# Attention backward on one core: dq columns as a stream of four a head, and dV three heads ahead of dK

## The chip, the cores and the metric

The kernel runs on one core of a Trainium2 chip. Its time is in microseconds of the device, the median of several executions. Besides it there is one profiled execution, from which all views of the trace come; its span is counted from the first to the last instruction. The engines are named as the profile names them: PE (TensorE, with PEld for its weight loads), DVE (VectorE), ACT (ScalarE), POOL (GpSimd) and SP (SyncE, which here only issues DMAs).

## The reference

One decode step of a transformer block is computed forward and then backward. The forward part, cut to what matters:

```python
# x [4,1,512], k_cache and v_cache [4,32,4096,128], all bf16
q = (layernorm(x) @ wq) per head                  # 4 x 32 heads of 128
p = softmax(q . k_cache * 128**-0.5)              # over 4096 keys
o = p . v_cache
h = x + o @ wo
out = h + (silu(hn @ w1) * (hn @ w3)) @ w2        # hn = layernorm(h)
```

The outputs are `out` and the gradients of x, k_cache, v_cache, wq, wo, w1, w3 and w2 for a given `grad_out`. For one head, with dO the gradient of its output o:

- dV = p (x) dO, an outer product of 4096 x 128 (1 MB in bf16)
- dS = p * (dO . V - c) * scale, with c = dO . o
- dK = dS (x) q, again 4096 x 128
- dq = scale * (M^T dO - c * kP), where M is the sum over keys of p * v k^T and kP the sum of p * k, both made in the forward part; dq then gives the gradients of wq and x.

## The kernel before

There are 128 heads (4 batches by 32), numbered s = 0 to 127. The keys and values of a head are 1 MB each. The front (lines 604 to 676) reads all K and V once and computes, a pair of heads at a time, scores, softmax (P_all), the matrix M of each head (128 x 129 in fp32) and kP. A middle stretch (lines 678 to 924) does the output projection, the second layernorm, the feed-forward part and its backward, down to dO of the first 32 heads (page 0), and makes dV of heads 0 and 1. The back (from line 927) reads all V a second time and writes dK and dV of all heads, and does all the rest beside that.

**Slots.** SBUF holds 23 slots of 1 MB (`Slot`, line 108), handed out from a queue of free ones. In the back, M occupies eight (16 heads each), the pages of wo up to four, one holds replicated rows, seven circulate among the second loads of V (`vring`, NV2 = 7, lines 789 to 798), and the others take dV and dK on their way out (`gv`, `gk`): such a slot is given back at once, and its next user waits for the DMA.

**The head pass.** `front(s)` (line 1161) turns the V of head s round: 32 transposes on PE in four batches, each evicted by ACT into the same slot (`V_T`, lines 757 to 765), then eight matmuls dO . V (line 1177), whose stationary operand `zd` POOL prepares two heads before (line 1142). After every fourth head the sums are evicted, transposed once more (lines 1152 and 1159), and `group_dS` (line 1185) makes dS of four heads on DVE.

**Outer products.** `grad_V(s)` (line 777) and `grad_K(s)` (line 1197) are one DVE instruction each (line 770), followed by a DMA of 1 MB on SP's queue (lines 781 and 1201). dV needs only P (pairs of P made by POOL, line 1147, three buffers) and the dO row of the head, replicated over the partitions; dK needs dS and the replicated q row. `replicate` (line 1121) makes such rows for four heads: four matmuls on PE into one PSUM buffer, one eviction on ACT.

**Order.** The program's order is written out by hand (lines 1233 to 1265), and each engine, SP's DMA queue among them, takes its own instructions in that order. Before the main loop, heads 0 to 4 pass `front`, and `more_V` (line 1212) makes dV of heads 2 to 8 between them. In the main loop over s, at each s: SP loads a further head of V into the slot that the last head pass set free; `front(s + 5)`; dV up to head s + 8 (`lead_V`, line 1224: the distance shrinks to 3 between heads 56 and 76); dK of head s; after every fourth head dS of the next four; one or more steps of work beside it.

**Work beside it.** It is written as generators and advanced by `step`. The generator "o" (line 1105, heads 2 to 20) transposes the remaining pages of wo and makes dO of heads 32 to 127, a page of 32 heads in six steps; its last step on a page has POOL put dO into `dOT_f` as fp32 (line 750). The generator "s" (`side_work`, line 951) begins at head 21 with three steps a head until head 35, then two. Its first 43 steps make dq: one fp32 matmul of 128 x 128 by one column for each head, three heads a step, so nine a head; every 16 heads one slot of M is given back, and after 64 and 96 heads a load of a quarter of wq is issued on SP's queue. What follows in "s" (dx, gradients of the weights, the output itself) takes about 150 steps.

Of the kernel before, what the change touches and what calls it, by code (L numbers as in the profile page):

```python
# [9 lines left out]
FP32 = mybir.dt.float32  # L10
# [14 lines left out]
def kernel(  # L25
# [22 lines left out]
    nc = tc.nc  # L48
    P = nc.NUM_PARTITIONS
# [5 lines left out]
    Dh = A_k_cache.shape[3]  # L55
    F = B_w1.shape[1]
    NH = B * H
    HD = H * Dh
    assert NH == P and Dh == P and H == 32 and Sk == 32 * P
    assert D == 4 * P and F % P == 0  # L60
    DC = D // P
# [5 lines left out]
    MC = 16  # L67
# [3 lines left out]
    x2 = A_x.rearrange("b s d -> (b s) d")  # L71
# [12 lines left out]
    def bh_of(s):  # L84
        return s % B, s // B

    def rows_of(ap):
        return ap.rearrange("(p j) d -> p j d", p=P)
# [74 lines left out]
    ident_b = const.tile([P, P], BF16, name="ident_b")  # L163
# [14 lines left out]
    def ones_window(col):  # L178
# [11 lines left out]
                          in_=rowg[:, None, :, None].to_broadcast([P, 4, 8, 4]))  # L190
# [70 lines left out]
    with ExitStack() as c0:  # L261
# [11 lines left out]
        for h in range(H):  # L273
            for cc in range(DC):
                nc.tensor.matmul(qT_ps[:, h, :], lhsT=wq_s[cc].b(HD)[:, h * Dh:(h + 1) * Dh], rhs=xhatT[:, cc, :],
                                 start=(cc == 0), stop=(cc == DC - 1))
# [4 lines left out]
        for r in range(2):  # L281
            for t_ in range(2):
                for q in range(4):
                    nc.tensor.matmul(qr_ps[32 * q:32 * (q + 1), 2 * r + t_, :], lhsT=ident_b[:, 64 * r + t_:64 * (r + 1):2],
                                     rhs=qT_bf[:], start=True, stop=True, tile_position=(0, 32 * q))
# [3 lines left out]
    Ms = []  # L289

    def M_of(s):
        return Ms[s // MC].f(MC * (Dh + 1)).rearrange("p (n c) -> p n c", c=Dh + 1)[:, s % MC, :]
# [305 lines left out]
    units = {"d": d_hh_units()}  # L598

    def step(k, n=1):  # L600
        for _ in range(n):
            next(units[k], None)
# [113 lines left out]
    dOT_f = pers2.tile([P, NH], FP32, name="dOT_f")  # L716
    dOrows_bf = pers2.tile([NH, Dh], BF16, name="dOrows_bf")
# [4 lines left out]
    qrows_bf = pers2.tile([NH, Dh], BF16, name="qrows_bf")  # L722
# [29 lines left out]
    REP = B  # L752
    reps = {}
# [13 lines left out]
    P2s, first_gv = {}, []  # L767
# [9 lines left out]
    def grad_V(s):  # L777
        b, h = bh_of(s)
        gv = Slot("gv")
        outer(gv.heads(), P2s.pop(s), reps["rdo", s // REP][:, s % REP, :])  # L780
        nc.sync.dma_start(out=rows_of(out_3[b, h]), in_=gv.heads())
        if s > 1:
            gv.give()
        else:
            first_gv.append(gv)
# [14 lines left out]
    with ExitStack() as cm:  # L800
# [33 lines left out]
        for wi, wt in enumerate((w1, w3)):  # L834
            for fc in range(FC):
                for cc in range(DC):
                    nc.tensor.matmul(gu_ps[:, wi, fc, :], lhsT=w13_view(wt, cc)[:, fc * P:(fc + 1) * P], rhs=hhatT[:, cc, :],
                                     start=(cc == 0), stop=(cc == DC - 1))
# [25 lines left out]
        for jj in range(DC):  # L864
            i_mm = 0
            for (lt, wt) in ((d_gateT_bf, w1), (d_upT_bf, w3)):
                for fc in range(FC):
                    nc.tensor.matmul(dn_ps[:, jj, :], lhsT=w13_view(wt, jj)[:, fc * P:(fc + 1) * P], rhs=lt[:, fc, :],
                                     start=(i_mm == 0), stop=(i_mm == 2 * FC - 1))
                    i_mm += 1  # L870
        for sl in w1 + w3:
            sl.give()
        rs = Slot("reps")
        rep_bufs = {nm_: [rs.b()[:, (2 * k + i) * 512:(2 * k + i + 1) * 512].rearrange("p (i d) -> p i d", i=REP) for i in range(2)]
                    for k, nm_ in enumerate(("rq", "rdo"))}
# [4 lines left out]
        ps = psA.tile([P, REP, Dh], FP32, tag="rT", name="repq_ps")  # L880
# [4 lines left out]
        for s in range(3):  # L885
# [8 lines left out]
                         start=True, stop=True)  # L894
# [14 lines left out]
        for b0, b1 in ((0, 1), (1, B)):  # L909
            ps = psA.tile([P, B, Dh], FP32, tag="rT", name="rep_ps")  # L910
            for b in range(b0, b1):
                for jj in range(DC):
                    nc.tensor.matmul(ps[:, b, :], lhsT=dhT[:, jj, b:b + 1].to_broadcast([P, P]), rhs=wo_page(0)[:, 0, jj, :],
                                     start=(jj == 0), stop=(jj == DC - 1))
# [12 lines left out]
    with ExitStack() as c2:  # L927
        psT = c2.enter_context(tc.tile_pool(name="psT2", bufs=2, space=bass.MemoryType.PSUM))
        psD = c2.enter_context(tc.tile_pool(name="psD", bufs=1, space=bass.MemoryType.PSUM))
        psrep = c2.enter_context(tc.tile_pool(name="psrep", bufs=1, space=bass.MemoryType.PSUM))  # L930
        psg = c2.enter_context(tc.tile_pool(name="psg", bufs=2, space=bass.MemoryType.PSUM))
        psx = c2.enter_context(tc.tile_pool(name="psx", bufs=1, space=bass.MemoryType.PSUM))
# [15 lines left out]
            gu.append((dst, ps, n))  # L948


        def side_work():
            pt = psg.tile([P, Dh], BF16, tag="gps", name="pt_O")
            nc.tensor.transpose(pt[:], OT_bf[:], ident_b[:])
            nc.scalar.copy(out=O_sb[:], in_=pt[:])
            dq_ps = psx.tile([P, 512], FP32, tag="x2", name="dq_ps")
            wq2s = deque()

            def load_wq2(cc):
                if cc < DC:
                    wq2s.append(Slot("wq2"))  # L960
                    nc.sync.dma_start(out=wq2s[-1].b(HD), in_=A_wq[cc * P:(cc + 1) * P, :])

            for s in range(NH):
                nc.tensor.matmul(dq_ps[:, s:s + 1], lhsT=M_of(s)[:, 0:Dh], rhs=dOT_f[:, s:s + 1], start=True, stop=True)
                if s % MC == MC - 1:
                    Ms[s // MC].give()
                    if s // MC in (3, 5):
                        load_wq2(s // MC // 2 - 1)
                if s % 3 == 2:
                    yield  # L970
            yield
            t = rs.f(2080)[:, 1536:1536 + NH]
            nc.vector.tensor_tensor(out=t, in0=c_rep[:], in1=kPT[:], op=ALU.mult)
# [13 lines left out]
            for cc in range(DC):  # L987
                wq2 = wq2s.popleft()
# [8 lines left out]
                for h in range(H):  # L997
                    nc.tensor.matmul(dx_ps[0:B, cc * P:(cc + 1) * P], lhsT=dqT_bf[:, h * B:(h + 1) * B], rhs=wv[:, h, :],
                                     start=(h == 0), stop=(h == H - 1))
# [62 lines left out]
            for i in range(2):  # L1062
                st = Slot("gw2")
                hw = hh_rows[:, i * 7 * P:(i + 1) * 7 * P].rearrange("b (p k) -> b k p", k=7)
                for k in range(7):
# [4 lines left out]
                                  in_=st.b(7 * D).rearrange("p (c j) -> p c j", c=7))  # L1070
# [4 lines left out]
            for (rows, out_ap) in ((dg_rows, out_6), (du_rows, out_7)):  # L1075
                for i in range(2):
                    st = Slot("gw13")
                    nw = hhat_bf[0:B, i * 2 * P:(i + 1) * 2 * P].rearrange("b (p k) -> b k p", k=2)
                    for k in range(2):
                        for (f0_, w_) in f_chunks:  # L1080
# [5 lines left out]
                                      in_=st.b(2 * F).rearrange("p (c f) -> p c f", c=2))  # L1086
                    st.give()
            r1.give()
            for h0 in range(0, H, 8):
                st = Slot("gwo")  # L1090
                ow = oflat.b(HD)[0:B, h0 * P:(h0 + 8) * P].rearrange("b (p k) -> b k p", k=8)
                for k in range(8):
# [4 lines left out]
                                  in_=st.b(8 * D).rearrange("p (k j) -> p k j", k=8))  # L1097
# [20 lines left out]
            nc.scalar.copy(out=dh, in_=dr_ps[:])  # L1118

        units["o"] = rest_of_dO()  # L1120
        def replicate(nm_, i0):
            if i0 >= NH or (nm_, i0 // REP) in reps:
                return
            K_ = 8 * B if i0 < 8 * B else P
            rows = dOrows_bf if nm_ == "rdo" else qrows_bf
            ps = psrep.tile([P, REP, Dh], FP32, tag="rep", name="rep_ps")
            for i in range(REP):
                nc.tensor.matmul(ps[:, i, :], lhsT=ident_b[0:K_, i0 + i:i0 + i + 1].to_broadcast([K_, P]), rhs=rows[0:K_, :],
                                 start=True, stop=True)
            rt = rep_bufs[nm_][i0 // REP % 2]  # L1130
            nc.scalar.copy(out=rt, in_=ps[:])
            reps[nm_, i0 // REP] = rt

        rows = {}
        dS2s = {}
# [8 lines left out]
        def P_pairs(s):  # L1144
            if s < NH and s not in P2s:
                P2s[s] = bw3.tile([P, SJ, 2], BF16, tag="P2", name="P2")
                nc.gpsimd.tensor_copy(out=P2s[s][:], in_=P_all[:, s, :, None].to_broadcast([P, SJ, 2]))  # L1147
# [13 lines left out]
        def front(s):  # L1161
            hl = s % B
            if s not in VTs:
                for g in range(SJ // GW):
                    V_T(s, psT, range(g, g + 1))
                    if hl == 0 and g == 0:
                        rows_out()
                    if hl == 0 and g == 2:
                        rows_T()
            VT = VTs[s].heads()  # L1170
            if hl == 0:
                rows["acc"] = psD.tile([P, 512], FP32, tag="dP", name="dP_ps")
            dO_window(s + 2)
            for u in range(2):
                for c in range(4):
                    j0 = 8 * c + 4 * u
                    nc.tensor.matmul(rows["acc"][32 * c:32 * (c + 1), :], lhsT=zq_window(zd[hl], 2 * hl + u),  # L1177
                                     rhs=VT[:, j0:j0 + 4, :], start=(hl == 0 and u == 0),
                                     stop=(hl == B - 1 and u == 1), tile_position=(0, 32 * c))
            if hl == B - 1:  # L1180
                rows["ps"] = rows.pop("acc")
            sl = VTs.pop(s)
            (vring if len(V2s) + len(VTs) + len(vring) < NV2 else free).append(sl.i)
# [22 lines left out]
                load_V2(nc.sync)  # L1206


        O0, S0, L = 2, 21, 5
        gvd = {"n": 2}  # L1210

        def more_V(upto):
            while gvd["n"] < min(NH, upto):
                s = gvd["n"]
                P_pairs(s)
                replicate("rdo", s - s % REP)
                grad_V(s)
                P_pairs(s + 1)
                P_pairs(s + 2)
                gvd["n"] += 1  # L1220
                if s % REP == 2:
                    replicate("rdo", s + 2)

        def lead_V(s):
            return 8 - min(5, max(0, s - 56) // 4)


        def load_ahead(s):
            prefetch()
            if s < NH and s not in V2s and s not in VTs:  # L1230
                load_V2(nc.sync)

        for s in range(2):
            dO_window(s)
        for s in range(3, 6):
            P_pairs(s)
        for s in range(L):
            load_ahead(s)
            front(s)
            if s == 0:  # L1240
                for gv in first_gv:
                    gv.give()
            more_V((4, 6, 7, 8, 9)[s])
            if s == 0:
                replicate("rdo", REP)
        group_dS(0)
        for s in range(NH):
            load_ahead(s + L)
            if s % REP == 2:
                replicate("rq", s + 2)  # L1250
            if s + L < NH:
                front(s + L)
            elif s + L == NH:
                rows_out()
                rows_T()
            if s > 0:
                more_V(s + 1 + lead_V(s))
            grad_K(s)
            if s % B == B - 1 and s + 1 < NH:
                group_dS((s + 1) // B)  # L1260
            if s >= S0:
                step("s", 3 if s < S0 + 15 else 2)
            elif s >= O0:
                step("o")
        step("s", 400)


# [28 lines left out]
```

## Time and profile before

| | |
|---|---|
| median of 3 runs | 1703.83 us (1702.63 to 1705.36) |
| profiled execution | 1702.63 us |
| its span | 1700.7 us |
| PE busy | 1258.0 us (74%) |
| DVE busy | 1236.7 us (73%) |
| ACT busy | 967.2 us (57%) |
| POOL busy | 397.8 us (23%) |
| moved by DMA | 707.50 MB, mean 416 GB/s |
| HBM read, written | 422.59 MB, 282.34 MB |
| second V load, dV, dK | 128 DMAs of 1 MB each |

The page cuts the span into 40 slices of 42.5 us and gives for each the busy tenths of the engines, of the 16 DMA engines and the GB/s moved. The front fills slices 0 to 15, the back begins in slice 16 near 703 us, and its main loop near 726 us. Views by window give, for a stretch, the time in it, the busy time of PE, PEld, DVE, ACT and POOL with the number of instructions, then the granted clock of PE, the DMA share and GB/s. Views in order of time give start, duration, engine, line, operation and count of merged instructions, and in brackets the idle time before and what ended it. For an instruction of SP, the duration is that of the issue, not of the transfer; the landing of each transfer is told by its semaphore.

### The profile page before, as it was taken

How to read it: one execution, taken by the hardware profiler on the slowest of the kernel's cores; microseconds unless marked ns; L12 is line 12 of the kernel's file. 1: busy time of each engine (PE TensorE's matmuls, PEld its weight loads, DVE VectorE, ACT ScalarE, POOL GpSimd, SP SyncE). 2: the span in 40 equal slices, each digit the busy share in tenths (PEclk: the TensorE clock that was granted, in tenths of full speed). 3: DMA queues.
4: the chain of work that ended last, by engine and by line, in shares of the span. 5: the costliest groups of instructions: out<-in, count | busy, mean ns of one | idle time of the engine just before them, and what ended most of it. 6: DMA issues, size and time to landing. Idle time of an engine off the chain costs nothing. (4 is left out here: it accounts for less than half of the span.)

```text
span 1700.7 us, 38400 instructions
## 1 busy us (share of the span) xinstructions
PE 1258.0 (74%) x16180; PEld 931.3 (55%) x16180; DVE 1236.7 (73%) x1294; ACT 967.2 (57%) x1502; POOL 397.8 (23%) x678
## 2 busy tenths in 40 slices
PE   5889888888888888877689877676577666666660
PEld 4777776666666666644467655443344343443440
DVE  5989899999998997667676676675465666665672
ACT  3555444544454444687754567676577666666550
POOL 1211222222222231323122352031022233200210
PEclk9999999999999999899976789988787877777665
DMA  9999999999999999999999999999999999999996
GB/s 401 424 425 423 424 424 424 423 424 424 414 424 411 422 406 401 385 419 425 425 425 426 425 424 425 425 426 426 424 422 422 419 421 415 419 421 410 412 425 280
DMA packets 101741, 707.50 MB, mean 416 GB/s; under 512 B 11052, under 2 KB 15288, under 8 KB 17600
## 3 DMA queue, kind: packets, MB, share of 16 engines
q1 hardware_dynamic: 101152, 704.95, 99.4%
q8 instruction: 127, 2.08, 0.5%
q14 instruction: 46, 0.38, 0.1%
q0 software_dynamic: 416, 0.10, 0.0%
HBM read 422.59 MB, written 282.34 MB: 414 GB/s over the span
## 5 line engine op out<-in xcount | busy, mean ns | idle before, releaser
L765 ACT COPY V<-pt_tps 128x1024 bf16<-128x1024 bf16 x512 | 490.5, 1027 | 168.0 <-PE pt_tps L764 158.7
L764 PE MATMUL pt_tps<-ident_b,V 128*128 128x128 bf16 x4096 | 361.8, 250 | 150.1 <-ACT V L765 93.1
L764 PEld LDWEIGHTS <-V 128*128 128x128 bf16 x4096 | 308.4, 114 | 258.3 <-issue 169.7
L770 DVE TENSOR_TENSOR gv<-P,reps 128x4096 bf16<-128x4096 bf16 x125 | 286.1, 2292 | 172.1 <-DMA out_dram<-gv 132.8
L770 DVE TENSOR_TENSOR gk<-dS,reps 128x4096 bf16<-128x4096 bf16 x128 | 293.4, 2294 | 111.1 <-DMA out_dram<-gv 77.3
L421 DVE TENSOR_TENSOR PK<-Kn,PK 128x4096 bf16<-128x4096 bf16 x128 | 292.3, 2283 | 26.1 <-POOL PK L417 25.7
L436 PE MATMUL M_ps<-PK,Vn 128*128 128x130 bf16 x4096 | 285.3, 222 | 33.9 <-DMA Vn<-in_A_v_cache_dram 33.4
L436 PEld LDWEIGHTS <-Vn 128*128 128x128 bf16 x4096 | 253.1, 99 | 53.8 <-DMA Vn<-in_A_v_cache_dram 45.7
L328 DVE STREAM_TRANSPOSE KT<-Kn 128x512 f32<-128x512 f32 (+1 forms) x321 | 250.6, 797 | 0.3 <-issue 0.2
L323 ACT COPY KT<-pt_tps 128x1024 bf16<-128x1024 bf16 x128 | 129.4, 1012 | 186.2 <-PE pt_tps L322 150.5
L1177 PE MATMUL dP_ps<-V,zd 128*32 128x512 bf16 x1024 | 179.1, 432 | 68.6 <-ACT V L765 65.8
L1147 POOL COPY P<-P_all 128x64 bf16<-128x64 bf16 x125 | 92.4, 740 | 468.7 <-DVE gv L770 468.6
L1142 POOL COPY zd<-dOT_bf 128x2 bf16<-128x2 bf16 x128 | 130.5, 1021 | 156.3 <-PE dP_ps L1177 156.3
L334 POOL TENSOR_TENSOR W<-qrep,wmask 128x128 bf16<-128x128 bf16 x128 | 123.7, 966 | 82.4 <-PE S_ps L354 67.6
L417 POOL COPY PK<-P_all 128x64 bf16<-128x64 bf16 x128 | 32.5, 254 | 414.6 <-ACT P_all L411 411.6
L1177 PEld LDWEIGHTS <-zd 128*32 128x32 bf16 x1024 | 37.2, 95 | 156.3 <-issue 141.7
L411 ACT COPY P_all<-pt_P 32x64 bf16<-32x64 bf16 x256 | 51.9, 203 | 53.4 <-PE pt_P L407 51.2
L322 PE MATMUL pt_tps<-ident_b,Kn 128*128 128x128 bf16 x1024 | 80.5, 223 | 0.0
L446 PE MATMUL kP_ps<-PK,onesw 128*32 128x512 bf16 x1024 | 79.1, 386 | 0.0
L322 PEld LDWEIGHTS <-Kn 128*128 128x128 bf16 x1024 | 62.0, 100 | 25.8 <-issue 25.8
L386 ACT ACTIVATE E<-S_ps,nm 128x256 f32<-128x256 f32 x64 | 30.3, 474 | 80.1 <-DVE nm L383 80.1
L400 ACT ACTIVATE Pn<-E,rl 128x1024 bf16<-128x1024 f32 x64 | 73.7, 1152 | 3.3 <-DVE rl L397 3.2
(239 smaller groups left out, 1244.8 us busy)
## 6 DMA issues: line engine op xcount, KB each, us to landing
Kn<-in_A_k_cache_dram SPq DMA_DIRECT2D x128, 1024.0 KB, 15.3
Vn<-in_A_v_cache_dram SPq DMA_DIRECT2D x128, 1024.0 KB, 15.8
V<-in_A_v_cache_dram SPq DMA_DIRECT2D x128, 1024.0 KB, 20.0
out_dram<-gv SPq DMA_DIRECT2D x128, 1024.0 KB, 20.0
out_dram<-gk SPq DMA_DIRECT2D x128, 1024.0 KB, 20.1
wq<-in_A_wq_dram SPq DMA_DIRECT2D x8, 1024.0 KB, 15.7
out_dram<-gw SPq DMA_DIRECT2D x6, 896.0 KB, 19.9
wo<-in_A_wo_dram SPq DMA_DIRECT2D x4, 1024.0 KB, 11.4
```

The lines of the kernel that those rows point to most:

```text
L322: nc.tensor.transpose(pt[:, i, :], Kn[:, c * GW + i, :], ident_b[:])
L323: nc.scalar.copy(out=KT[:, c * GW:(c + 1) * GW, :], in_=pt[:])
L328: nc.vector.transpose(out=KT[:, c * w_:(c + n) * w_], in_=Kn[:, c * w_:(c + n) * w_])
L334: nc.gpsimd.tensor_tensor(out=W[:, hl], in0=qrep[:, :, s:s + 1].to_broadcast([P, 4, 32]), in1=wmask[:, hl, None, :].to_broadcast([P, 4, 32 ...
L421: nc.vector.tensor_tensor(out=PK[:, :, 0:Dh].rearrange("p j (r t) -> p j r t", t=2), in0=Ks[s].heads().rearrange("p j (r t) -> p j r t", t=2),
L436: nc.tensor.matmul(hold["M"][:], lhsT=Vn[:, j, :], rhs=PK[:, j, :], start=(j == 0), stop=(j == SJ - 1))
L764: nc.tensor.transpose(pt[:, i, :], v[:, g * GW + i, :], ident_b[:])
L765: nc.scalar.copy(out=v[:, g * GW:(g + 1) * GW, :], in_=pt[:])
L770: nc.vector.tensor_tensor(out=dst.rearrange("p j (r t) -> p j r t", t=2), in0=col2[:, :, None, :].to_broadcast([P, SJ, Dh // 2, 2]), in1=r ...
L1142: nc.gpsimd.tensor_copy(out=zd[s % B][:, 32:132:67], in_=dOT_bf[:, s:s + 1].to_broadcast([P, 2]))
L1147: nc.gpsimd.tensor_copy(out=P2s[s][:], in_=P_all[:, s, :, None].to_broadcast([P, SJ, 2]))
L1177: nc.tensor.matmul(rows["acc"][32 * c:32 * (c + 1), :], lhsT=zq_window(zd[hl], 2 * hl + u), rhs=VT[:, j0:j0 + 4, :], start=(hl == 0 and u ...
```

## The change

Two things are rewritten. The dq columns leave `side_work` and become a generator "q" of their own, with four heads a step and one step at each head from 2 to 33; the two first loads of wq are issued after 96 and 112 heads of it. `side_work` begins at head 35 with two steps a head. And dV is no longer made up to eight heads ahead: before the main loop dV of heads 2 and 3 is made, and in the loop dV of head s + 3 beside dK of head s. With it go `more_V` and `lead_V`; the replicated rows of dO and q for four heads are now made together, at every fourth head, and P's pairs are made once at each head, five heads ahead.

```diff
+        wq2s = deque()
+
+        def load_wq2(cc):
+            if cc < DC:
+                wq2s.append(Slot("wq2"))
+                nc.sync.dma_start(out=wq2s[-1].b(HD), in_=A_wq[cc * P:(cc + 1) * P, :])
+
+        dq_ps = psx.tile([P, 512], FP32, tag="x2", name="dq_ps")
+
+        def dq_work():
+            for s in range(NH):
+                nc.tensor.matmul(dq_ps[:, s:s + 1], lhsT=M_of(s)[:, 0:Dh], rhs=dOT_f[:, s:s + 1], start=True, stop=True)
+                if s % MC == MC - 1:
+                    Ms[s // MC].give()
+                    if s // MC in (5, 6):
+                        load_wq2(s // MC - 5)
+                if s % 4 == 3:
+                    yield
+
+        units["q"] = dq_work()
+
         def side_work():
...
-            for s in range(NH):
-                nc.tensor.matmul(dq_ps[:, s:s + 1], lhsT=M_of(s)[:, 0:Dh], rhs=dOT_f[:, s:s + 1], start=True, stop=True)
-                if s % MC == MC - 1:
-                    Ms[s // MC].give()
-                    if s // MC in (3, 5):
-                        load_wq2(s // MC // 2 - 1)
-                if s % 3 == 2:
-                    yield
             yield
...
-        def replicate(nm_, i0):
-            if i0 >= NH or (nm_, i0 // REP) in reps:
-                return
+        def replicate(i0):
             K_ = 8 * B if i0 < 8 * B else P
-            rows = dOrows_bf if nm_ == "rdo" else qrows_bf
-            ps = psrep.tile([P, REP, Dh], FP32, tag="rep", name="rep_ps")
...
+            for nm_, rows in (("rdo", dOrows_bf), ("rq", qrows_bf)):
+                if (nm_, i0 // REP) in reps:
+                    continue
+                ps = psrep.tile([P, REP, Dh], FP32, tag="rep", name="rep_ps")
...
-        O0, S0, L = 2, 21, 5
-        gvd = {"n": 2}
-
-        def more_V(upto):
-            while gvd["n"] < min(NH, upto):
-                s = gvd["n"]
-                P_pairs(s)
-                replicate("rdo", s - s % REP)
-                grad_V(s)
-                P_pairs(s + 1)
-                P_pairs(s + 2)
-                gvd["n"] += 1
-                if s % REP == 2:
-                    replicate("rdo", s + 2)
-
-        def lead_V(s):
-            return 8 - min(5, max(0, s - 56) // 4)
-
+        O0, S0, S1, L, LV = 2, 21, 35, 5, 3
...
         for s in range(2):
             dO_window(s)
-        for s in range(3, 6):
-            P_pairs(s)
         for s in range(L):
             load_ahead(s)
+            P_pairs(s)
             front(s)
-            if s == 0:
-                for gv in first_gv:
-                    gv.give()
-            more_V((4, 6, 7, 8, 9)[s])
-            if s == 0:
-                replicate("rdo", REP)
+            if s < 2:
+                first_gv[s].give()
+            elif s < LV + 1:
+                grad_V(s)
         group_dS(0)
         for s in range(NH):
             load_ahead(s + L)
-            if s % REP == 2:
-                replicate("rq", s + 2)
+            if s % REP == 0 and s + REP < NH:
+                replicate(s + REP)
+            P_pairs(s + L)
             if s + L < NH:
                 front(s + L)
             elif s + L == NH:
                 rows_out()
                 rows_T()
-            if s > 0:
-                more_V(s + 1 + lead_V(s))
+            if s > 0 and s + LV < NH:
+                grad_V(s + LV)
             grad_K(s)
             if s % B == B - 1 and s + 1 < NH:
                 group_dS((s + 1) // B)
-            if s >= S0:
-                step("s", 3 if s < S0 + 15 else 2)
+            if O0 <= s < S0:
+                step("o")
+            if s >= S1:
+                step("s", 2)
             elif s >= O0:
-                step("o")
+                step("q")
         step("s", 400)
```

More of the change, by code (lines that the diff above doesn't have):

```diff
@@ L954, in side_work @@
             nc.scalar.copy(out=O_sb[:], in_=pt[:])
[L955 to L961, printed above, removed]
-            for s in range(NH):
-                nc.tensor.matmul(dq_ps[:, s:s + 1], lhsT=M_of(s)[:, 0:Dh], rhs=dOT_f[:, s:s + 1], start=True, stop=True)
-                if s % MC == MC - 1:
-                    Ms[s // MC].give()
-                    if s // MC in (3, 5):
-                        load_wq2(s // MC // 2 - 1)
-                if s % 3 == 2:
-                    yield
             yield
@@ L1120 @@
         units["o"] = rest_of_dO()
-        def replicate(nm_, i0):
-            if i0 >= NH or (nm_, i0 // REP) in reps:
-                return
+        def replicate(i0):
             K_ = 8 * B if i0 < 8 * B else P
-            rows = dOrows_bf if nm_ == "rdo" else qrows_bf
-            ps = psrep.tile([P, REP, Dh], FP32, tag="rep", name="rep_ps")
[L1127 to L1132, printed above, removed]
+            for nm_, rows in (("rdo", dOrows_bf), ("rq", qrows_bf)):
+                if (nm_, i0 // REP) in reps:
+                    continue
+                ps = psrep.tile([P, REP, Dh], FP32, tag="rep", name="rep_ps")
+                for i in range(REP):
+                    nc.tensor.matmul(ps[:, i, :], lhsT=ident_b[0:K_, i0 + i:i0 + i + 1].to_broadcast([K_, P]), rhs=rows[0:K_, :],
+                                     start=True, stop=True)
+                rt = rep_bufs[nm_][i0 // REP % 2]
+                nc.scalar.copy(out=rt, in_=ps[:])
+                reps[nm_, i0 // REP] = rt
         rows = {}
```

## The prediction

> **What bounds the kernel now.** I read the page's slices first, then ten-microsecond windows around the seam between front and back, then the issues of SP and the work of VectorE in order of time, last the end.
>
> ```profile
> DMA  9999999999999999999999999999999999999996
> GB/s 401 424 425 423 424 424 424 423 424 424 414 424 411 422 406 401 385 419 425 425 425 426 425 424 425 425 426 426 424 422 422 419 421 415 419 421 410 412 425 280
> ```
>
> The DMA engines are full in every slice but the last, at 424 to 426 GB/s where nothing disturbs them, while no other engine passes 74% of the span. 707.5 MB at 425 GB/s are 1665 us of the 1700.7, so the time is bytes over rate plus what DMA stands idle. Slice 16 (680 to 723 us), the seam before the loop that writes dK and dV, is the lowest but for the end.
>
> ```profile
> 700.00:710.00 10.00, 6.97 (x65) 4.89 (x63) 7.96 (x8) 5.76 (x8) 3.38 (x13) 0.66 0.86 356
> 710.00:720.00 10.00, 6.95 (x84) 4.46 (x83) 9.58 (x5) 7.72 (x9) 7.74 (x7) 1.00 1.01 418
> 720.00:730.00 10.00, 7.00 (x79) 4.38 (x77) 6.66 (x8) 7.49 (x10) 4.44 (x5) 1.00 0.99 361
> 730.00:740.00 10.00, 7.15 (x84) 4.39 (x82) 5.09 (x4) 7.76 (x10) 1.35 (x5) 1.00 1.00 423
> 740.00:750.00 10.00, 7.55 (x86) 4.79 (x86) 7.08 (x7) 7.76 (x11) 2.56 (x3) 1.00 1.02 425
> ...
> 1650.00:1675.00 25.00, 3.91 (x28) 2.27 (x27) 14.46 (x11) 3.53 (x5) 0.00 (x0) 0.57 1.01 426
> 1675.00:1700.00 25.00, 0.00 (x0) 0.00 (x0) 0.00 (x0) 0.00 (x0) 0.00 (x0) 0.50 0.45 189
> ```
>
> The last three columns are granted clock, DMA share and GB/s. From 730 us on DMA is never idle until 1685. After that only one of the 16 engines' worth (27 GB/s) moves until 1699: one engine lags, and it ends the kernel. By the landings in the trace, transfers of 1 MB land from 732 to 1699.4 us every 2.51 us on average (385 gaps), with no gap over 3.2 us. So whatever delays the start of this unbroken run delays the end, one for one, and engines other than DMA matter only where they let it run dry.
>
> ```profile
> 700.74 16.61 SPq L781 DMA_DIRECT2D out_dram<-gv  x7
> 717.46 0.78 SPq L797 DMA_DIRECT2D V<-in_A_v_cache_dram  x1
> 719.22 0.33 SPq L781 DMA_DIRECT2D out_dram<-gv  x1
> 721.81 0.34 SPq L797 DMA_DIRECT2D V<-in_A_v_cache_dram  x1
> 722.25 0.53 SPq L781 DMA_DIRECT2D out_dram<-gv  x1
> 727.34 0.34 SPq L797 DMA_DIRECT2D V<-in_A_v_cache_dram  x1
> 728.24 0.33 SPq L1201 DMA_DIRECT2D out_dram<-gk  x1
> 732.33 0.34 SPq L797 DMA_DIRECT2D V<-in_A_v_cache_dram  x1
> ```
>
> ```profile
> 707.56 6.72 DVE L770 TENSOR_TENSOR gv<-P,reps 128x4096 bf16<-128x4096 bf16 x3
> 714.70 6.73 DVE L770 TENSOR_TENSOR gv<-P,reps 128x4096 bf16<-128x4096 bf16 x3 [0.42 <-POOL P L1147]
> 724.70 0.73 DVE L1191 TENSOR_SCALAR dPr<-dPT_ps,c_rep 128x32 f32<-128x32 f32 x4 [3.27 <-PE dPT_ps L1159]
> 725.92 2.29 DVE L770 TENSOR_TENSOR gk<-dS,reps 128x4096 bf16<-128x4096 bf16 x1
> ```
>
> The first are SP's issues in order of time (start, us of issuing, count merged), the second is VectorE. Nine dV writes (heads 0 to 8) leave between 700.7 and 722.3 us, before dS of the first group exists (724.7). They are what DMA has to do while PE and ScalarE turn heads 1 to 4 round, 5.0 us a head; the V loads alone come once in those 5 us and fill 2.5.
>
> **Part 1, dV no longer ahead at the start.** Before the main loop the changed kernel makes dV of heads 2 and 3 only, where it made 2 to 8. Five writes go, 5 x 2.51 = 12.55 us of DMA work, and are made later instead. VectorE loses nothing by it: 5 x 2.29 us lie in time it has. The main loop's order on SP is the old one (V load, dV, dK for each head; in the old kernel dV of head 9 stands where dV of head 4 will). So I follow the queue in the new order. dV 2 and 3 leave at 707.7 and 709.9 as now. The loads follow the ends of the head passes: 717.5 was held behind a dV issue, PE ended at 716.4; without the two replications in this stretch (0.39 us of PE, 0.58 of ACT, about 0.5 of pace each) the loads go at about 715.9, 721.1 and 726.3. dS comes 1 us earlier, dK 0 leaves at about 727.2. Then both replications of heads 4 to 7 stand back to back ahead of head 5, with one PSUM buffer between them (PE, ACT, PE, ACT: about 1.5 us), so head 5 ends, and the next load leaves, at about 732.8 instead of 732.33, with dV 4 and dK 1 right behind it. Each of these transfers takes 2.5 us, so DMA idles 0.7 + 3.3 + 2.7 + 2.7 + 1.6 = 11 us between 707 and 733, where the windows above show 2.9 (356, 418, 361 GB/s against 425, from 706 on). From 732.8 every 5 to 6 us bring three transfers, 7.5 us of work: full again.
>
> Counted by landings: that load landed at 742.20. On an idle queue a dV write took 4.0 to 4.7 us to land, so I put it at 737.3. It lands 4.9 us earlier, with 12.55 us of writes still owed: **+7.65 us**. Bounds: replications hidden and fastest landing (731.5 + 4.0 = 735.5) give +5.9; issue at 733.9 and the 6.72 us that a V load took after a quiet stretch give +10.9.
>
> **Part 2, dq as its own stream.** Removed: three dq steps a head from head 21 (18 PE instructions, two passes for each fp32 column, 2.12 us at full clock, 4.00 at half). Added: 8 instructions a head from 2 to 33.
>
> ```profile
> L964 PE MATMUL dq_ps<-dOT_f,M x256: 222/250/373, 866.7 to 986.8; 128*128 128x1 f32 x128
> ```
>
> 2.12 x 4/9 = 0.94 us of PE a head, now beside the wo units ("o" steps, heads 2 to 20), which pace the heads at 6.09 us (eight V evictions start from 744.4 to 787.0). That makes 7.03, or 6.5 where the wo eviction covers part of it; DMA needs 3 x 2.46 = 7.4. The cover holds, thinly: nothing added on the path. Heads 21 to 35 lose their bursts, but DMA was full through them, so nothing is gained. dq reads dOT_f, which GpSimd turns back page by page: pages end at about heads 7, 13, 19, and dq reaches them at 10, 18, 26, so no wait; were one there, PE's in-order stream would hold the next V transposes behind it.
>
> Half clock is the open price: at 895 a head pass with half clock took 6.2 us, dq would be 1.8, the wo transposes 1.1, waits 0.6: 9.7 a head. The clock was 0.95 from 740 to 862 and 0.73 from 862 to 1000, where dq ran in bursts. I take +0.5 us, for dips that hit while the queue is still short; bounds 0 and +13 (clock 0.8, so 40% of 19 heads at 9.7, less the short queue's cover).
> The Trainium skill (TensorE: Matmul & The Clock Gate, Part 1) says activity over windows of 3.4 us releases the throttle and idling brings half rate; the dips here last multiples of 3.41 us. By that rule thinly filled windows speak against mixing dq into the wo stage, and were all 19 heads at half clock, an estimate from the rows would be 19 x 2.3 = 44 us less the queue's cover.
>
> **Part 3, the rest, at nothing.** The four wq columns' loads keep their number; the first two leave at heads 25 and 29 instead of 28 and 31, in a full queue. M's eight slots are free from head 5 to 33 instead of 22 to 36, so writes have more room; before, four slots already kept DMA full (VectorE's waits on dV landings are the ring's own). Side work starts at head 35 one half head later than it stood, and ends near head 112 of 128. P's pairs on GpSimd now wait for dV two heads back and stand ahead of zd, three iterations' slack instead of four; uncovered, it would hold PE's dP matmuls, but VectorE is 4.6 of 7.4 us busy. The lead was 3 from head 76 on anyway, so the end is the old one.
> One small gain: while fewer than eight transfers are under way three land in 7.37 us (740 to 800), later in 7.55 to 7.6 (from 860, all landings 20 us after issue). The new queue starts shorter and reaches 20 us perhaps seven heads later: 7 x 0.2 = **-1 us** (0 to -3).
>
> **Sum:** +7.65 + 0.5 - 1.0 = +7.2 us. The profiled execution (1702.63, span 1700.7) would be 1709.8; against the median, 1.2 us above it, **1711 us**.
>
> **Rivals.** *PE becomes the bound* in heads 2 to 20: for it the 0.73 clock beside dq, against it that four columns make 0.9 us of a 3.4 us stretch, not 2.1. At clock 0.8 it adds some 10 us: 1720. *The gap is hidden anyway:* loads or dK start earlier than I chain them. For it: PE waits on ScalarE, so the pace has some slack; against: V slots come free only as heads are turned. Half the price: 1705. *The queue stays shallow (faster):* if the spread-out dq keeps PE nearly as slow as DMA, landings stay at 2.456 us instead of 2.53. It pays back 0.22 us a head and wins once it lasts 34 heads longer than before; over 80 heads it gives -17 + 7.65, 1694. Against: after head 20 the pace is 6 us a head, and the queue must fill. That the lead is not really cut is excluded by the text: head s + 3 is the furthest.
>
> **Chances.** Forecast 0.70 (1707 to 1715), PE bound 0.14, hidden 0.11, shallow 0.05. About 0.2%, 3.4 us, can be told from no change. Slower takes the first two and a bit of the third: 0.86; within, 0.10; faster 0.04. The range reaches down into the hidden case and up to the PE case: 1705 to 1720.
>
> **What would show it.** Right: between 710 and 733 us a DMA share near 0.55, three dV and dK issues instead of eight, full from about 733, landings 2.5 us apart to the end, the tail as now. Part 2 is right if DMA stays at 425 GB/s from 740 to 860. Wrong: no deeper hole at the seam (hidden); holes between 740 and 860 with low granted clock (PE); landing times under 15 us past head 30 (shallow).

## The result, and the profile after

The median after is 1712.53 us (1711.25 to 1715.62, four runs) against 1703.23 for the kernel before on the same chip (four runs): ratio 1.0055, 95% interval 1.0038 to 1.0073, **9.3 us slower**. The profiled execution took 1712.23 us, its span 1710.3 (+9.6 on the 1700.7 of before). Ratios here and below leave out runs more than 1.5% above the fastest of their own kernel, which concerns only the two kernels with four slots (two runs of twelve, one of six) and makes their ratios a little low.

The slices of the page after, 42.8 us each:

```profile
DMA  9999999999999999799999999999999999999996
GB/s 401 424 424 424 424 423 425 423 424 424 415 424 411 421 408 399 311 381 425 425 426 425 425 425 426 425 426 426 426 423 421 420 422 421 421 422 415 417 418 283
```

Two slices have changed, 16 and 17 at the seam: 311 and 381 GB/s for 385 and 419. From slice 18 on the rate is close to that of before, up to the end. The windows of 30 us over the hole, the stretch in which DMA lacks work, show it best, first of the kernel before, then after (window, its length, busy time and count of PE, PEld, DVE, ACT and POOL, then granted clock, DMA share, GB/s):

```profile
710.00:740.00 30.00, 21.10 (x242) 13.22 (x241) 21.33 (x15) 22.97 (x27) 13.52 (x15) 1.00 1.00 401
```

```profile
710.00:740.00 30.00, 20.82 (x245) 13.35 (x241) 12.47 (x10) 22.61 (x26) 6.59 (x11) 1.00 0.73 237
```

PE and ACT do the same work at the same pace. VectorE does five instructions less, some 9 us, and DMA moves (401 - 237) x 30 us = 4.9 MB less. That is 11.6 us at 425 GB/s. But only 27% of 30 us = 8.1 us of it are idle by the share. The other 3.5 us passed while transfers were under way and moved slowly. In smaller windows of the kernel after:

```profile
700.00:710.00 10.00, 6.80 (x59) 4.40 (x56) 7.34 (x7) 5.92 (x7) 5.58 (x13) 0.66 0.89 366
710.00:720.00 10.00, 6.95 (x85) 4.32 (x80) 0.00 (x0) 7.52 (x8) 0.72 (x4) 1.00 0.36 113
720.00:730.00 10.00, 6.87 (x85) 4.69 (x81) 6.53 (x8) 7.55 (x10) 2.01 (x4) 1.00 0.88 301
730.00:740.00 10.00, 7.00 (x84) 4.33 (x82) 5.93 (x3) 7.54 (x9) 3.86 (x4) 1.00 0.95 296
740.00:750.00 10.00, 8.01 (x90) 5.48 (x87) 5.67 (x7) 7.24 (x9) 2.43 (x2) 1.00 1.01 424
750.00:860.00 110.00, 88.64 (x965) 66.96 (x964) 73.53 (x54) 74.79 (x85) 39.52 (x32) 0.86 1.01 425
860.00:1000.00 140.00, 104.53 (x1106) 74.30 (x1105) 102.12 (x77) 96.04 (x113) 59.82 (x47) 0.93 1.01 425
...
1685.00:1710.00 25.00, 0.00 (x0) 0.00 (x0) 0.00 (x0) 0.00 (x0) 0.00 (x0) 0.50 0.44 185
```

Look at 730 to 740: a share of 0.95 at the full pace would be 404 GB/s, and 296 were moved. From 740 on all is as before, and the tail (0.44 and 185 GB/s) is the old one, 10 us later. SP's issues in order of time (start, us of issuing, count merged) and VectorE's work after:

```profile
700.19 7.27 SPq L781 DMA_DIRECT2D out_dram<-gv  x3
715.42 0.34 SPq L797 DMA_DIRECT2D V<-in_A_v_cache_dram  x1
715.85 0.38 SPq L781 DMA_DIRECT2D out_dram<-gv  x1
720.41 5.87 SPq L797 DMA_DIRECT2D V<-in_A_v_cache_dram  x2
726.82 0.34 SPq L1206 DMA_DIRECT2D out_dram<-gk  x1
732.31 0.33 SPq L797 DMA_DIRECT2D V<-in_A_v_cache_dram  x1
732.73 0.38 SPq L781 DMA_DIRECT2D out_dram<-gv  x1
733.20 0.38 SPq L1206 DMA_DIRECT2D out_dram<-gk  x1
```

```profile
707.40 2.29 DVE L770 TENSOR_TENSOR gv<-P,reps 128x4096 bf16<-128x4096 bf16 x1 [0.30 <-DMA out_dram<-gv]
723.28 0.73 DVE L1196 TENSOR_SCALAR dPr<-dPT_ps,c_rep 128x32 f32<-128x32 f32 x4 [13.60 <-PE dPT_ps L1164]
```

VectorE now waits 13.6 us for the sums of the first four heads, where it waited 3.3. All it could have written meanwhile, dV 4 to 8, has been put off. SP issues between 707.5 and 726.8 us three loads of V and one dV, and nothing else.

How far the delay carries is read from the landings: the time of the n-th landing of a large transfer (1 MB or 896 KB, counted from 0), less that in the kernel before (us). The 290th lands near 737 us there, the 310th near 786, the 410th near 1039, the 510th near 1291, the 630th near 1592.

```
n      290   310   330   350   370   390   410   470   570   630   last
after  11.7  12.0  11.2  11.0  11.3  11.8  10.7  10.6  10.0   9.6   9.6
```

The whole loss is there by the 290th landing (12.1 us at most, near the 304th). Nothing more is added later, and 2.1 us come back.

### The profile page after: what moved, and what is told of

Same layout as the page of the kernel before. It is cut to its first block, busy times and chain, and to the rows that moved or that the text cites. A ratio compares the mean times of both kernels' runs of the same rounds, so it can differ in the third digit from the quotient of the medians.

```text
span 1710.3 us, 38409 instructions
## 1 busy us (share of the span) xinstructions
PE 1252.7 (73%) x16180; PEld 924.1 (54%) x16180; DVE 1235.5 (72%) x1294; ACT 969.1 (57%) x1502; POOL 424.2 (25%) x680
## 5 line engine op out<-in xcount | busy, mean ns | idle before, releaser
L1152 POOL COPY P<-P_all 128x64 bf16<-128x64 bf16 x127 | 126.5, 996 | 536.2 <-DVE gv L770 528.9
L1182 PE MATMUL dP_ps<-V,zd 128*32 128x512 bf16 x1024 | 184.3, 440 | 67.1 <-ACT V L765 64.1
L1147 POOL COPY zd<-dOT_bf 128x2 bf16<-128x2 bf16 x128 | 125.2, 978 | 63.8 <-PE dP_ps L1182 63.8
L1136 ACT CAST reps<-rep_ps 128x512 bf16<-128x512 f32 x62 | 36.4, 587 | 89.9 <-DVE gk L770 56.7
## 6 DMA issues: line engine op xcount, KB each, us to landing
wo<-in_A_wo_dram SPq DMA_DIRECT2D x4, 1024.0 KB, 11.7
```

What stands on the lines that cost most here:

```text
L1147: nc.gpsimd.tensor_copy(out=zd[s % B][:, 32:132:67], in_=dOT_bf[:, s:s + 1].to_broadcast([P, 2]))
```

## The experiments

Theory at the outset: the loss is dV's order alone, through the writes that DMA lacks at the seam, and the dq stream costs nothing. Rivals: dq has a share in it, or gives something back; a later part of the shorter lead has a share; the queue's depth after the seam decides what is lost or regained. All ratios are to the kernel before on the same chip, with their 95% interval.

**dq alone.** The kernel before with the dq stream (generator "q" and `side_work` from head 35 as in the change's diff), and `more_V` and `lead_V` left as they were:

```diff
-            if s >= S0:
-                step("s", 3 if s < S0 + 15 else 2)
-            elif s >= O0:
+            if O0 <= s < S0:
                 step("o")
+            if s >= S1:
+                step("s", 2)
+            elif s >= O0:
+                step("q")
```

> Only the dq columns move into their own stream (four a head from head 2 to 33); dV stays up to eight heads ahead. Theory (the hole at the seam is the whole loss, dq lies beside other work): 1703 us, within 3 us of the kernel before, DMA full from 730 us on, no hole between 710 and 733. Rival (dq beside the wo units slows PE and lets the queue run dry): 1706 or more, with DMA under 420 GB/s somewhere between 740 and 900.

Measured: 1702.74 us, 0.9997 [0.9989, 1.0006]. The seam and the stretch with dq beside the wo units in it:

```profile
710.00:720.00 10.00, 7.56 (x83) 4.88 (x81) 9.47 (x5) 7.54 (x9) 5.83 (x6) 0.93 0.98 403
720.00:730.00 10.00, 7.36 (x84) 4.71 (x84) 6.78 (x8) 7.49 (x10) 4.55 (x5) 1.00 1.01 358
730.00:740.00 10.00, 6.99 (x82) 4.23 (x80) 6.88 (x4) 7.76 (x9) 3.54 (x6) 1.00 1.01 425
...
750.00:860.00 110.00, 87.87 (x1006) 65.70 (x1003) 80.41 (x65) 78.57 (x90) 33.47 (x33) 0.93 1.01 425
```

PE has 87.9 us of work in 110 us, 76.8 before, and DMA stays at 425. The dq stream is worth nothing either way.

**dV alone.** The kernel after with dq back in `side_work`, three heads a step from head 21:

```diff
-        units["q"] = dq_work()
...
-            if O0 <= s < S0:
-                step("o")
-            if s >= S1:
-                step("s", 2)
+            if s >= S0:
+                step("s", 3 if s < S0 + 15 else 2)
             elif s >= O0:
-                step("q")
+                step("o")
```

> Only dV's order changes (two heads before the main loop, then three ahead, with the joint replication); dq stays nine a head from head 21. Theory: 1711 to 1714 us, as the whole change, with the hole between 710 and 740. Rival (the loss comes from dq): 1703 to 1706. If the spread-out dq gives something back (the whole change lost 11.7 us at the seam and ended only 9.6 us later), this one is 1 to 3 us slower than the whole change.

Measured: 1712.77 us, 1.0054 [1.0041, 1.0066], the time after. All of the loss comes with the change of dV's order.

**Lead of three in the old order.** The change also moved the replications, P's pairs and dV 3's place on SP. The kernel before with only the distance cut:

```diff
         def lead_V(s):
-            return 8 - min(5, max(0, s - 56) // 4)
+            return 3
...
-            more_V((4, 6, 7, 8, 9)[s])
+            more_V((4, 4, 4, 4, 4)[s])
```

> The kernel before with only the distance of dV cut to three heads throughout; replication and the pairs of P stay where they were, so dV of head 3 is issued ahead of the next V load. Theory: the five writes that are missing at the seam are what counts: 1710 to 1713 us. Rival (the joint replication, the pairs of P and dV 3 behind the V load make the loss): 1707 or less.

Measured: 1713.73 us, 1.0061 [1.0048, 1.0073]. The order of the rest costs nothing that shows; with the lead alone cut, five writes fewer at the seam, the whole loss is there.

**Lead of five.** Two of the five writes back at the seam:

```diff
-            return 8 - min(5, max(0, s - 56) // 4)
+            return 5 - min(2, max(0, s - 56) // 4)
...
-            more_V((4, 6, 7, 8, 9)[s])
+            more_V((4, 5, 6, 6, 6)[s])
```

> The kernel before with dV up to five heads ahead instead of eight (heads 2 to 5 before the main loop), so three writes are missing at the seam instead of five. Theory (each missing write costs about 2 to 2.5 us): 5.5 to 7 us over the kernel before, 1709 to 1710. Rival (a threshold: the cost comes from one wait that any shorter distance triggers): as the cut to three, or as before.

Measured: 1709.07 us, 1.0033 [1.0021, 1.0045], +5.7 by the medians. Three missing writes cost 5.7 and five 10.3 (in the old order): 1.9 to 2.1 us a write, somewhat under the 2.51 that one takes.

```profile
710.00:720.00 10.00, 6.95 (x83) 4.29 (x81) 3.71 (x2) 7.49 (x9) 4.31 (x5) 1.00 0.99 392
720.00:730.00 10.00, 7.00 (x79) 4.23 (x77) 7.68 (x8) 7.94 (x9) 3.15 (x3) 1.00 0.72 272
730.00:740.00 10.00, 6.86 (x82) 4.44 (x80) 4.69 (x3) 8.12 (x10) 2.85 (x4) 1.00 0.99 356
```

The hole now begins 10 us later and is shallower, and again its last window shows a share of 0.99 with 356 GB/s only: the slow stretch comes right behind the idle one here too. A slow stretch does not need an idle one, though: the kernel before has 361 GB/s at a share of 0.99 from 720 to 730 us, with a share of 1.01 ahead of it.

**A lead of eleven at the start.** If the seam is closed at eight, more writes bring nothing:

```diff
-            return 8 - min(5, max(0, s - 56) // 4)
+            return (11 if s < 12 else 8) - min(5, max(0, s - 56) // 4)
...
-            more_V((4, 6, 7, 8, 9)[s])
+            more_V((4, 6, 8, 10, 12)[s])
```

> The kernel before with dV up to eleven heads ahead at the seam (heads 2 to 11 before the main loop) and until head 11, then eight. Theory (at eight the hole is closed: DMA share 0.99 to 1.0 from 710 on): nothing more to fill, 1702 to 1705 us. Rival (every write moved ahead of dS is worth 2 us, as from three to five to eight): 1697 to 1700.

Measured: 1703.79 us, 1.0000 [0.9991, 1.0009].

**Fewer slots for dV and dK** (four kernels). The prediction let a shorter queue land transfers faster. Here the slots that dV and dK leave by are held to W, so that a new one waits for the oldest, and the queue stays short for good; `grad_K` is edited as `grad_V`. W = 4, 5 and 3 in the kernel before, and W = 4 in the kernel after:

```diff
+    def out_slot(nm_):
+        if outn["n"] < W and free:
+            outn["n"] += 1
+            return Slot(nm_)
+        return Slot(nm_, out)
...
-        gv = Slot("gv")
+        gv = out_slot("gv")
...
-            gv.give()
+            out.append(gv.i)
```

> The kernel before, but dV and dK use four slots in rotation throughout (before, they take whatever slot is free, up to some fifteen), so about six transfers are under way instead of eight. Theory (a full queue is what lets one DMA engine fall five transfers behind; the whole change gained back 2 us by filling its queue later): the lag at the end falls from 5 transfers to 1 or 2, landings stay near 2.46 us, 1694 to 1700 us. Rival (the lag comes from work that the engine has in any case, such as instruction loads): the lag at the end stays near 5 and the time within 2 us of before. Third (too shallow): DMA share falls under 1.0 in the main loop, slower.

> As four slots, with five. Theory: between, lag 2 to 4, 1697 to 1702. Rival: as before.

> The changed kernel with four slots in rotation. The seam's hole is untouched, so it stays 8 to 11 us over the same limit on the kernel before; if the limit gains 5 us there, 1704 to 1709 here.

> The kernel before with three slots in rotation, about four to five transfers under way. Theory: if four already suffice to keep DMA full, three is near the edge: DMA share under 1.0 in places, 1700 to 1720. Rival: the same as four.

Measured: W = 4 1.0095 [1.0060, 1.0131], with single runs from 1706.96 to 1735.58 us; W = 5 1.0087 [1.0069, 1.0105]; W = 4 in the kernel after 1.0108 [1.0079, 1.0136]; W = 3 1.0258 [1.0243, 1.0273]. None is faster; the gain that a short queue was to bring is not there. Two windows of the kernel with four slots, then one of the kernel with three:

```profile
750.00:860.00 110.00, 72.28 (x862) 47.46 (x861) 71.10 (x56) 76.34 (x89) 27.17 (x32) 0.93 1.01 425
...
1000.00:1300.00 300.00, 196.81 (x2066) 128.16 (x2065) 178.99 (x131) 204.07 (x248) 47.55 (x83) 0.86 1.00 408
```

```profile
750.00:860.00 110.00, 69.16 (x793) 45.94 (x790) 65.84 (x54) 72.41 (x83) 8.03 (x30) 0.91 1.01 391
```

With four, the landings keep the pace of before up to 1000 us (0.6 to 1.6 us behind it all the way) and fall back from about 1140 on, 408 GB/s where the kernel before has 424. With three, the share says 1.01 and 391 GB/s are moved: a packet of 8 KB takes 336 ns on average there, 310 in the kernel before. From 750 to 860 us some 6.3 transfers are under way on average in the kernel before, 5.3 with four slots and 3.7 with three. With four the packets are as fast as before (310 ns) and with three slower; in none does a shorter queue make a full stream land faster.

**The lead paid back at once.** The kernel before makes its eight writes at the seam and then loses the lead over heads 1 to 5 rather than 56 to 76:

```diff
-            return 8 - min(5, max(0, s - 56) // 4)
+            return max(3, 8 - s)
```

> The kernel before with dV of heads 2 to 8 before the main loop as it is, but no dV at heads 1 to 5, so that from head 5 on dV is three ahead. Theory (what counts is that DMA always has work): the hole at the seam is closed, but heads 1 to 5 bring two transfers (5.0 us) in 5.0 to 6.4 us of head pass with a short queue, so part of the hole opens there: 1705 to 1710 us, with DMA under 400 GB/s between 740 and 765. Rival (only the stretch before dS counts): 1702 to 1705.

Measured: 1704.47 us, 1.0007 [0.9998, 1.0016]. The 1705 to 1710 looked for was too high: giving the lead up behind the seam costs this kernel some 1 us at most. The short hole that it makes at heads 1 to 5 is there, and the landings are 3.2 us late behind it, but at the end only 0.9:

```profile
750.00:760.00 10.00, 6.69 (x77) 4.24 (x75) 6.73 (x4) 8.77 (x10) 2.15 (x3) 1.00 1.02 397
760.00:770.00 10.00, 7.11 (x109) 4.92 (x109) 1.73 (x3) 6.69 (x9) 0.36 (x2) 1.00 1.00 378
```

**The seam filled in the kernel after.** dV of heads 2 to 7 before the loop instead of 2 and 3, so four of the five missing writes, and a lead of three from then on:

```diff
-            if s < 2:
-                first_gv[s].give()
-            elif s < LV + 1:
-                grad_V(s)
+            if s == 0:
+                for gv in first_gv:
+                    gv.give()
+            for i in ((2, 3), (4, 5), (6,), (7,), ())[s]:
+                P_pairs(i)
+                grad_V(i)
+            if s == 0:
+                replicate(REP)
...
-            if s > 0 and s + LV < NH:
+            if s + LV > 7 and s + LV < NH:
                 grad_V(s + LV)
```

> The changed kernel with dV of heads 2 to 7 before the main loop (four of the five writes back at the seam) and none at heads 1 to 4, so that from head 5 on dV is three ahead as in the change; dq as a stream of its own. Theory (the hole at the seam is the whole loss): 1703 to 1706 us, DMA share near 1.0 from 710 on. Rival (in the changed kernel something else holds the time, a distance of three in the loop or dq beside the wo units): 1709 or more.

Measured: 1709.56 us, 1.0033 [1.0021, 1.0046]; 3 us regained of 9, where 6 to 9 were looked for. That is the time that the rival forecast (1709 or more: something else in the changed kernel holds it), so this run does not bear out that filling the seam is enough there. The landings are 3.4 us late at the 290th and 9.7 at the 310th. In the windows of it the hole has moved to where heads 1 to 4 of the loop bring two transfers each instead of three:

```profile
750.00:760.00 10.00, 7.80 (x79) 5.46 (x79) 8.44 (x9) 7.89 (x10) 3.09 (x2) 0.83 0.97 336
760.00:770.00 10.00, 7.80 (x96) 5.93 (x96) 3.99 (x2) 6.97 (x8) 1.54 (x3) 1.00 0.95 363
770.00:780.00 10.00, 8.33 (x103) 6.23 (x102) 5.79 (x9) 6.54 (x8) 0.00 (x0) 0.83 1.00 378
```

**dq and the lead paid back at once.** Is it dq's 0.94 us a head on PE, in just those heads, that makes this hole deeper? The dq-alone kernel with the lead of the last but one:

```diff
-            return 8 - min(5, max(0, s - 56) // 4)
+            return max(3, 8 - s)
```

> The kernel before with dV of heads 2 to 8 before the main loop, none at heads 1 to 5, and dq as a stream of its own (the two edits of which each alone changed the time by 1.3 us or less). It asks why the changed kernel with its seam filled stayed at 1709.6. Theory A (dq lengthens the head pass by up to 1 us at heads 2 to 5, just where each head brings two transfers and the queue is near empty): 1707 to 1711 us, with DMA under 380 GB/s between 745 and 775. Theory B (four writes instead of five, and the joint replication, made the rest): 1703 to 1706.

Measured: 1704.73 us, 1.0004 [0.9995, 1.0013]. dq with the early pay-back is not enough for it. This kernel has a hole of like depth (385 and 335 GB/s from 750 to 770 us; without dq it was 397 and 378) and gets most of it back, 6.4 us behind at its worst and 2.5 at the end of the profiled execution. The filled kernel after has one write less before the loop, both replications at once at head 4, and another order; its seam also started 2 us late in the profiled execution. Which of these holds its remaining 6 us was not told apart.

## Why the prediction was right, and which of its terms were off

**The bound** held: the DMA engines are never idle from 740 us to the tail, and most of a delay at the seam is a delay of the end. Lead of three (+10.3), five (+5.7), eight (0) and eleven (0) show it: what the seam lacks is lost, and what it has too much of brings nothing.

**Part 1, issue by issue.** The loads left at 715.42, 720.41, 725.94 and 732.31 us (put at 715.9, 721.1, 726.3, 732.8), dK 0 at 726.82 (727.2): each within 0.7 us. dV 3 was missed: it left at 715.85, not 709.9, since in the new program a load of V that waits for head 2's pass stands ahead of it on SP. It fell into a gap anyway, and the lead of three in the old order, with dV 3 ahead of that load, is no faster. Of the signs named, the three dV and dK issues between 710 and 733 us are there, the DMA share there is 0.67 where about 0.55 was named, and DMA is full from 740 us, not from 733. The 11 us and the 2.9 of before count full-rate time not used, so they are checked by GB/s. From 707 to 733 us the kernel after moved 237 GB/s and the kernel before 378, so that 11.5 and 2.9 us at 425 GB/s were not used: 8.6 us added, put at 8.1. But from 733 to 740 us, put down as full, it moved 282 GB/s (before 426), and 2.4 us more were lost. Together that is 11.0 of the 11.7 us by the landings.

**The term that was mis-sized** is how fast the last load before the full run lands: put at 737.3 us, 4.5 us after its issue by the dV writes, it landed at 741.40, after 9.09. So 0.8 us of the 12.55 were recovered and not 4.9: +11.75 at that point for +7.65, past the upper bound of 10.9 too. The error was to take the queue as idle: dK 0, issued at 726.82, was under way until 735.60, and dV and dK were issued 0.4 and 0.9 us behind the load. Timing a load by a write was not in itself the error: in the kernel with a lead of three in the old order, two loads with nothing beside them landed 4.72 and 4.80 us after their issue, hardly later than a write. With one write under way beside it, or issued within 0.9 us behind it, a load took 6.56 to 6.60 us in the kernel after (those of 715.42, 720.41 and 725.94) and 5.09 to 6.92 in the others with a hole. With a write ahead of it and two right behind, as for the load in question, it took 9.09 us here, 9.10 in the old order, and 7.11 to 8.50 in three others. The row of 6.72 us that the upper bound was taken from, the load of 694.55 in the kernel before, was not after a quiet stretch either: two loads were still landing, until 696.49 and 698.80, and another was issued 0.43 us behind it.

Packets of 8 KB, 309 ns in the full stream, took 325 to 1020 ns on average in the six stretches of 2 us from 726 to 738, most in the one from 726 to 728 and next in those from 734 to 738 (650 and 534). That is the part of the hole that the share does not show. Why they are slow was not tested.

The Trainium skill (DMA: Bandwidth & Descriptors, Measured) gives 6.15 us for a 1 MB load, as DMA busy time of transfers issued by GpSimd. The loads with nothing beside them here, from SP's queue and counted from the issue, took less, 4.72 and 4.80 us, and what is measured here decides.

**Part 2** at nothing: shown by dq alone (0.9997). The +0.5 us for half clock was not spent: the clock was 0.86 from 750 to 860 us and DMA at 425. **Part 3**: -1 us was put down, and 2.1 came back between the 290th landing and the last. But the reason given, faster landings in a queue not yet full, is not borne out: with four slots the queue was kept short and no landing came faster. It rests on a misread pace. The trace has 16 increments for each transfer, and the last one counts as its landing. In the kernel before, the last increments of three transfers take 7.36 us from 740 to 800 us and 7.59 from 860 to 1000, but the middle ones of the 16 only 7.39 and 7.44, at 425 GB/s in both. So most of the slower landings is one engine that falls behind (see the last section), and not a deeper queue. The price of the shallow rival rested on the same pace. That four slots keep DMA full held in the four-slot kernel up to 1000 us and not behind it. Two other kernels with a lead of three regained 1.6 (the old order) and next to nothing (dV alone), so the 2 us may be of these executions; their cause stays open.

**The sum** of +7.2 against +9.6 in the profiled executions: seam 4.1 too little, clock 0.5 too much, recovery 1.1 too little (7.2 + 4.1 - 0.5 - 1.1 = 9.7). The mechanism and the place of the loss were right; that the sum came so near is in part luck, since a seam term beyond its own bound was offset in part by a recovery whose reason did not hold. The seam term also scatters: at the 290th landing the three profiled kernels with a lead of three are 8.8 (dV alone), 11.7 and 12.7 us late (the old order), and at the end 9.1, 9.6 and 11.1. The rivals fell: a PE bound by 425 GB/s beside dq, a hidden gap by the share of 0.73, a queue that stays shallow and is faster by all four kernels with fewer slots.

## What to carry to other kernels

Where DMA is full but for one seam, what counts is how many bytes are ready to move while the seam's own chain runs: count them as writes per head pass, and put into that gap work that needs nothing from the chain. A lead is worth just what fills the gap (here five writes; eleven heads ahead do no more than eight). The kernel before could give it up at once behind the gap for some 1 us; the changed one, with four of the five writes, still ended 6.5 us behind, for reasons not told apart. Price a hole from bytes not moved (GB/s), not from the idle share, and do not time its end by a transfer on an idle queue: ask what else is under way or issued right behind.

## What the runs showed that was not expected

- The DMA share can read full while the rate falls. With three slots for dV and dK it was 1.01 at 391 GB/s, and 0.95 at 296 GB/s where the queue started again after the hole. In both few transfers are under way (3.7 on average with three slots); the link is a correlation, it does not hold for four slots from 750 to 1000 us (5 to 6 under way, 425 GB/s), and its cause was not tested.
- A deeper queue seems to be a cushion. With some eight transfers under way the kernel before holds 425 to 426 GB/s from 862 to 1225 us; with four slots (five to six under way) it was 425 up to 1000 us and 408 from 1000 to 1300, and the runs scatter by 29 us.
- One of the 16 engines falls behind the others. By the last of a transfer's 16 increments against the middle ones, at 2.46 us a transfer, it is 0.8 transfers behind near 730 us in the kernel before, 2.2 near 1000, 4.7 near 1300 and about 5.5 from 1400 on. It makes the tail of some 12 us at 27 GB/s, after the other engines have ended (1687.6 us). With four slots it is 1.2 behind near 1690 us, but that kernel is slower. Why one engine lags, and why less there, is open.
